# Shared key/value buffers in a gated mix of attention and a feed-forward net, and an earlier step for odd chunks' down weights

## The chip, the cores and the metric

The kernel runs on one core of one Trainium2 chip. A run's time is the device time of one execution, in microseconds (us), and less is better. The kernel before takes 601.78 us, the median of 3 runs (601.47 to 602.52). Each profiled execution also has a span, from its first to its last recorded instruction. The engines are TensorE (PE in the profile; its weight loads are PEld), VectorE (DVE), ScalarE (ACT), GpSimd (POOL) and SyncE (SP), which here only issues DMAs.

## The reference

Everything is in float32; x has 2048 rows of 512 columns.

```python
qkv = x @ wqkv                          # 32 heads of 16
idx = pos[:, None] - 2 * arange(8)      # 8 keys: this row and every second one behind it
logits = einsum("bhsd,bhswd->bhsw", q, k[idx]) * scale      # masked where idx < 0
o = einsum("bhsw,bhswd->bhsd", softmax(logits), v[idx])
a = o @ wo
b = (gelu(x @ w_gate) * (x @ w_up)) @ w_down                # 1792 hidden columns
g = sigmoid((x * gate_w).sum(-1))
out = g * a + (1 - g) * b
```

A row sees only keys at even distances, so even rows and odd rows never meet.

## The kernel before

The rows are split into two **parities** (`par` 0 and 1, even and odd rows, 1024 each), which go through the same stages one after the other: the projection of x to queries and keys; then `ffn(par)`, the feed-forward net in 14 chunks of 128 hidden columns (`f` = 0 to 13). In chunks 0 and 1 of `ffn` the pieces between the products are the projection to values (L130, banks `acc`); in later chunks they are the down projection of the two chunks before (L475, `down`). At the end stands the output projection (L693, L733 and after). By the trace the first projection lies at about 0 to 45 us, `ffn(0)` at 45 to 281, the second projection at 281 to 345, `ffn(1)` up to about 543, and the output projection behind it.

**Matmuls.** A float32 product is written as three matmuls of rounded halves: hi by hi, hi by lo, lo by hi. So each operand is split into `hi` (the rounded value) and `lo` (the rest). A chunk has seven block products of six matmuls each (L432, `product`), with sums of blocks in the place of an eighth product. Every matmul has a moving operand of 512 columns.

**The weights of a chunk.** The gate and up weights come as `raw` (SP, L360 and L361), VectorE makes block sums (L371 to L374, `combine`), and `operands` makes the halves in two groups, `g0` and `g1`: ScalarE writes minus hi into the lo half (L389), GpSimd issues a DMA that adds `raw` to it (L390, `g<-raw`, an accumulating DMA), and ScalarE writes hi (L394). The down weights go the same way in `down_w`: L418 on ScalarE, the accumulating DMA `d<-r` on GpSimd (L419), then L421 on ScalarE. For parity 1 `g0` comes back from DRAM (L385); `g1` and `d` are made again. `do` and `at(i, ...)` in `ffn` say at which of nine steps of a chunk's program each of these is written: step 0 is the chunk's head, step 8 its end.

**The hidden values.** ScalarE copies a product out of PSUM (`s`, L437), VectorE adds (`c`, L442), multiplies the gate and the up part (L446), ScalarE rounds (`hh`, L448), VectorE subtracts (`hl`, L449). `hh` and `hl` are the stationary operands of the down projection.

**Attention** runs on VectorE beside all this. A parity has four **units** (`u` = 0 to 3, 128 of the 512 channels), and a unit takes: keys and queries in (`load_kq`, L185), scores (L212 product and L215 sum, four times each, then L219, a minimum with the mask for the first rows, the last operation of a unit's scores), softmax (L226 to L236), the gate (L244, L246), values in (`mix`, L253), and the weighted sum (L260 to L268). It is written as a generator that is pulled forward a little at a time between the products, with lower priority. Keys lie in `2 * NP - 1` = 15 slots per partition (448 KB and 512 KB in two DMAs, L196 and L197), queries in 8 (512 KB, L193).

**Buffers.** `kq` (15 slots of keys and 8 of queries) and `v` (15 slots of values) have one buffer each. Unit 0 of a parity has its keys and queries written straight into `kq` by the projection (`take_first`, `shift`); the other units load them from DRAM. So a unit's keys can be loaded once the unit before has had its last L212, and a unit's values once the mix before is done.

**Order.** A scheduler orders each engine's queue from the program's order, priorities and a few written dependencies: `paced` makes an instruction wait for the last matmul written before it, `after` makes one instruction wait for another through a semaphore, `ordered` only fixes the order in a queue. An engine takes its queue strictly in order, so an instruction that waits holds all behind it. That goes for SP and GpSimd, which issue the DMAs, too.

Of the kernel before, what the change touches and what calls it, by code (L numbers as in the profile page):

```python
# [10 lines left out]
F32 = mybir.dt.float32  # L11
F32R = mybir.dt.float32r
AF = mybir.ActivationFunctionType
OP = mybir.AluOpType
AX = mybir.AxisListType

P = 128
S, D, F = 2048, 512, 1792
# [11 lines left out]
UC = 128  # L30
# [18 lines left out]
def tile_gated_mix(ctx: ExitStack, tc: tile.TileContext, xt, wqkv, wff, wo, out):  # L49
# [22 lines left out]
    zero = pool.tile([P, UC], F32, name="zero")  # L72
    nc.vector.memset(zero, 0.0)
    warm = zero.bitcast(mybir.dt.bfloat16)
    LAST = []
    idle = [bank("p") for _ in range(4)]
    for i in range(WARM):
        c = i // 4 % 2 * QW
# [57 lines left out]

    def take_first(par, ps, jj, copy):

        if par not in KQ:
            KQ[par] = pool.tile([P, 3 * NP - 1, UC], F32, name="kq")  # L140
        st = tl(next(stages))[:, :CU].rearrange("p (a d) -> p a d", a=2)
        two = ps.rearrange("p (a c d) -> p c a d", a=2, c=2)
        copy(KQ[par][:, NP - 1 + jj::NP], two[:, 0])
        copy(st, two[:, 1])
        for a, t in enumerate((KS[par, 0][1, W:], QS[par, 0][1])):
            nc.sync.dma_start(t.rearrange("(p j) d -> j p d", j=NP)[jj], st[:, a])

    def shift(par, queue, i, j):
        k = KQ[par][:, :2 * NP - 1]
        if not i:  # L150
            nc.gpsimd.memset(k[:1, :NP - 1], 0.0)
        for a, b in (1, P - 15), (P - 15, P):
            queue.dma_start(k[a:b, i:j], k[a - 1:b - 1, NP + i:NP + j])
# [28 lines left out]

    LG = {}

    def load_kq(par, u):  # L185
        hh, c = divmod(u, 2)
        kq = KQ[par] if not u else pool.tile([P, 3 * NP - 1, UC], F32, name="kq")
        k, q = kq[:, :2 * NP - 1], kq[:, 2 * NP - 1:]
        LG[par, u] = k, q
        if not u:  # L190
            return
        load_slots(k, KS[par, hh][c])
        nc.sync.dma_start(q, QS[par, hh][c].rearrange("(p j) d -> p j d", j=NP))  # L193

    def load_slots(t, src):
        nc.sync.dma_start(t[:, :NP - 1], src[:S // 2].rearrange("(p j) d -> p j d", j=NP)[:, 1:])  # L196
        nc.sync.dma_start(t[:, NP - 1:], src[W:].rearrange("(p j) d -> p j d", j=NP))  # L197

    def spans(t, jj):

# [6 lines left out]
    def scores(par, u):  # L207
        k, q = LG[par, u]
        lg = pool.tile([P, UH, NP, W], F32, name="lg", bufs=2)
        for jj in range(0, NP, 2):  # L210
            prod = pool.tile([P, 2, W, UC], F32, name="prod")
            paced(nc.vector.tensor_tensor(prod, spans(k, jj), q[:, jj:jj + 2, None, :].to_broadcast([P, 2, W, UC]),  # L212
                                          op=OP.mult))
            yield 2.3
            nc.vector.tensor_reduce(two_of(lg, jj), prod.rearrange("p j w (h d) -> p (j w) h d", d=DH), axis=AX.X,  # L215
                                    op=OP.add)
            yield 2.3
        first = lg[:1, :, :NP - 1, :W - 1]
        nc.vector.tensor_tensor(first, first, mask[:1, None, :NP - 1, :W - 1].to_broadcast([1, UH, NP - 1, W - 1]),  # L219
                                op=OP.min)  # L220
        LG[par, u] = lg

    def softmax(par, u):
# [25 lines left out]
    def mix(par, u, pause):  # L249
        lg = LG.pop((par, u))  # L250
        hh, c = divmod(u, 2)
        v = pool.tile([P, 2 * NP - 1, UC], F32, name="v")
        load_slots(v, VS[par, hh][c])  # L253
        yield pause
        tb = pool.tile([P, 2, BT * UC], F32, name="tb")
        for jj in range(0, NP, 2):
            if jj % BT == 0:
                o = pool.tile([P, 4, BT, 32], F32, name="o")
            prod = pool.tile([P, 2, W, UC], F32, name="prod")
            paced(nc.vector.tensor_tensor(prod.rearrange("p j w (h d) -> p (j w) h d", d=DH),  # L260
                                          spans(v, jj).rearrange("p j w (h d) -> p j w h d", d=DH),
                                          two_of(lg, jj)[:, :, :, None].to_broadcast([P, 2 * W, UH, DH]), op=OP.mult))
# [33 lines left out]
    def attention():  # L296
        units = [(0, u) for u in range(NU)] + [(1, u) for u in range(NU)]
        yield from need(0, 0)
        load_kq(0, 0)
        yield from scores(0, 0)  # L300
        load_kq(0, 1)
        yield from scores(0, 1)
        yield from need(0, 1)
        scored, mixed = 2, False
        for i, un in enumerate(units):
            if scored == i:
                yield from need(un[0], un[1] // 2 * 2)
                load_kq(*un)
                if un[1]:
                    yield LOAD  # L310
                yield from scores(*un)
                scored += 1
                mixed = False
            if un == (1, 0):
                load_kq(*units[scored])
            yield from softmax(*un)
            if un == (1, 0):
                yield from scores(*units[scored])
                scored += 1
                yield from need(un[0], 1)  # L320
            yield from gated(*un)


            to = units[scored] if scored < len(units) else None
            ahead = to and (to[0], to[1] // 2 * 2) in done
            if ahead:
                load_kq(*to)
            yield from mix(*un, LOAD if mixed else 0.0)
            done.add((*un, "o"))
            mixed = not ahead  # L330
            if ahead:
                yield from scores(*to)
                scored += 1
# [101 lines left out]
    def copy(ps):  # L435
        s = tl("s")
        COPIED[:] = [nc.scalar.activation(s, ps, AF.Copy)]  # L437
        return s
# [133 lines left out]
    def ffn(par):  # L572
# [3 lines left out]
        for f in range(FC):  # L576
# [10 lines left out]
            if f + 1 < FC:  # L587
# [7 lines left out]
                        at(3, down_split, g_)  # L595
                if f > 1:
                    steps = down_w(f)
                    at(2 if f > 2 else 4, next, steps, None)
                    at(7, next, steps, None)
            else:  # L600
                steps = down_w(f)
# [643 lines left out]
```

## Time and profile before

| | |
|---|---|
| median of 3 runs | 601.78 us (601.47 to 602.52) |
| the profiled execution, its own time | 602.86 us |
| its span | 601.0 us |
| TensorE busy | 591.8 us, 98% of the span, 2778 matmuls |
| VectorE busy | 531.1 us, 88% |
| ScalarE busy | 391.9 us, 65% |
| GpSimd busy | 89.3 us, 15% |
| moved by DMA | 134.18 MB, 223 GB/s on the mean |

The table's shares are means over the whole span. An engine's row in a timeline has the start, the duration, the engine, the line, the operation with what it writes and reads (`out<-in`), how many were merged into one row, and in brackets how long the engine sat idle before it and what ended that. A row of the list of waits has the engine, line and operand that waited, what it waited for, the total time in us, the number of waits and the longest. A row of the chain of waits is one step of the chain that ended last: start, duration, what. Matmuls are pipelined: the next starts before the one ahead ends, so the distance between starts, not the duration of one, says how fast they go.

### The profile page before, as it was taken

The numbers are of one execution on the slowest core, as the hardware profiler recorded it, in microseconds if no ns is written. First come the engines' busy times: TensorE is split into PE (matmuls) and PEld (weight loads), VectorE is DVE, ScalarE is ACT, GpSimd is POOL, SyncE is SP. The second block draws the span as 40 slices with busy tenths as digits, with TensorE's granted clock in tenths as the row PEclk, the third lists the DMA queues.
The fourth block names the chain that finished last, engine by engine and source line by source line (L and its number), as shares of the span: only waits on it lengthen the run. The fifth ranks groups of instructions, "written<-read, shape, count | busy, mean of one in ns | idle before, by whom it ended". The sixth has DMA issues, their size and how long they took to land.

```text
span 601.0 us, 8207 instructions
## 1 busy us (share of the span) xinstructions
PE 591.8 (98%) x2778; PEld 493.1 (82%) x2778; DVE 531.1 (88%) x618; ACT 391.9 (65%) x670; POOL 89.3 (15%) x121
## 2 busy tenths in 40 slices
PE   8999999999999999999999999999999999999997
PEld 6889987788888787888889988788888888888886
DVE  5997969999898897899989887999999988799862
ACT  6845657787678766787772375667667656885532
POOL 0501001111111111202026001111111111101300
PEclk9999999999999999999999999999999999999999
DMA  8789896999889989887879858597867877648924
GB/s 318 259 250 248 242 266 187 265 256 249 241 241 258 232 236 253 223 262 279 282 221 302 219 155 282 144 245 195 238 172 216 214 226 171 168 106 227 159 68 155
DMA packets 80449, 134.18 MB, mean 223 GB/s; under 512 B 8092, under 2 KB 46362, under 8 KB 80152
## 3 DMA queue, kind: packets, MB, share of 16 engines
q1 hardware_dynamic: 62890, 97.67, 50.3%
q0 software_dynamic: 12576, 32.97, 27.5%
q10 hardware_dynamic: 4942, 3.01, 1.6%
q8 instruction: 22, 0.36, 0.3%
q14 instruction: 19, 0.16, 0.1%
HBM read 68.30 MB, written 38.86 MB: 178 GB/s over the span
## 4 chain that ended last, share of the span: by engine, by line
PE 65%; DMA 12%; issue 11%; DVE 7%; ACT 2%; SPq 1%; POOL 1%; ACTq 0%; POOLq 0%; DVEq 0%
PE p L432 26%; PE p L475 9%; PE acc L475 8%; PE acc L760 6%; PE p L693 5%; PE p L760 5%; PE acc L130 4%; DMA d<-r 3%; DMA kq<-qs 3%; DMA ws<-g 3%; DVE prod L212 3%; PE acc L693 2%; DVE lg L215 1%; DMA g<-raw 1%; DMA vs<-hl 1%
## 5 line engine op out<-in xcount | busy, mean ns | idle before, releaser
L432 PE MATMUL p<-S,g 128*128 128x512 f32 x672 | 166.8, 390 | 0.5 <-ACT s L437 0.4
L432 PEld LDWEIGHTS p<-S,g 128*128 128x128 f32 x672 | 125.4, 188 | 27.2 <-ACT s L437 0.8
L432 PE MATMUL p<-A,g 128*128 128x512 f32 x504 | 127.2, 390 | 0.1
L432 PEld LDWEIGHTS p<-A,g 128*128 128x128 f32 x504 | 94.1, 188 | 20.6 <-DVE c L442 1.1
L212 DVE TENSOR_TENSOR prod<-kq 128x2048 f32<-128x2048 f32 x32 | 73.1, 2284 | 16.6 <-DMA kq<-qs 7.7
L390 POOL DMA_DIRECT2D g<-raw x40 | 34.6, 865 | 300.5 <-ACT g L389 230.1
L260 DVE TENSOR_TENSOR prod<-v,lg 128x2048 f32<-128x2048 f32 x32 | 72.9, 2277 | 2.3 <-DMA v<-vs 1.4
L215 DVE TENSOR_REDUCE lg<-prod 128x128 f32<-128x2048 f32 x32 | 73.0, 2281 | 0.2
L475 PE MATMUL p<-d,hh 128*128 128x512 f32 x224 | 68.1, 390 | 0.3 <-ACT hh L448 0.3
L475 PE MATMUL acc<-d,hh 128*128 128x512 f32 x224 | 60.7, 391 | 1.8 <-DMA d<-r 1.8
L475 PEld LDWEIGHTS acc<-d,hh 128*128 128x128 f32 x224 | 41.8, 188 | 11.6 <-DMA d<-r 2.6
L475 PEld LDWEIGHTS p<-d,hh 128*128 128x128 f32 x224 | 42.0, 188 | 9.5 <-ACT hh L448 0.8
L394 ACT ACTIVATE g<-raw 128x1024 fp32r<-128x1024 f32 (+1 forms) x40 | 39.5, 989 | 13.4 <-PE p L432 13.4
L389 ACT ACTIVATE g<-raw 128x1024 fp32r<-128x1024 f32 (+1 forms) x40 | 39.4, 985 | 10.9 <-PE p L760 4.6
L442 DVE TENSOR_TENSOR c<-p,s 128x512 f32<-128x512 f32 x56 | 38.0, 681 | 9.2 <-PE p L432 8.4
L448 ACT ACTIVATE hh<-c 128x512 fp32r<-128x512 f32 x56 | 35.0, 625 | 15.5 <-DVE c L446 15.0
L437 ACT ACTIVATE s<-p 128x512 f32<-128x512 f32 x56 | 33.1, 593 | 18.0 <-PE p L432 16.5
L475 PE MATMUL p<-d,hl 128*128 128x512 f32 x112 | 42.7, 390 | 1.0 <-DVE hl L449 1.0
L449 DVE TENSOR_TENSOR hl<-c,hh 128x512 fp32r<-128x512 f32 x56 | 38.3, 683 | 3.1 <-ACT hh L448 3.0
L446 DVE TENSOR_TENSOR c<-c 128x512 f32<-128x512 f32 x56 | 38.2, 682 | 2.1 <-ACT c L543 1.8
L264 DVE TENSOR_TENSOR prod<-prod 128x1024 f32<-128x1024 f32 x32 | 39.0, 1218 | 0.3
L491 ACT ACTIVATE rt<-p 128x512 f32<-128x512 f32 x48 | 28.2, 593 | 15.3 <-PE p L475 15.2
(180 smaller groups left out, 929.5 us busy)
## 6 DMA issues: line engine op xcount, KB each, us to landing
g<-raw POOLq DMA_DIRECT2D x27, 512.0 KB, 6.8
raw<-wff SPq DMA_DIRECT2D x42, 256.0 KB, 3.4
ws<-g SPq DMA_DIRECT2D x14, 768.0 KB, 6.1
g<-ws SPq DMA_DIRECT2D x14, 768.0 KB, 5.5
r<-wff SPq DMA_DIRECT2D x28, 256.0 KB, 4.3
d<-r POOLq DMA_DIRECT2D x24, 256.0 KB, 6.9
g<-raw POOLq DMA_DIRECT2D x13, 384.0 KB, 6.0
v<-vs SPq DMA_DIRECT2D x8, 512.0 KB, 5.7
```

The costliest lines, as they stand in the source:

```text
L212: paced(nc.vector.tensor_tensor(prod, spans(k, jj), q[:, jj:jj + 2, None, :].to_broadcast([P, 2, W, UC]), op=OP.mult))
L215: nc.vector.tensor_reduce(two_of(lg, jj), prod.rearrange("p j w (h d) -> p (j w) h d", d=DH), axis=AX.X, op=OP.add)
L260: paced(nc.vector.tensor_tensor(prod.rearrange("p j w (h d) -> p (j w) h d", d=DH), spans(v, jj).rearrange("p j w (h d) -> p j w h d", d=D ...
L264: nc.vector.tensor_tensor(prod[:, :, :4], prod[:, :, :4], prod[:, :, 4:], op=OP.add)
L389: nc.scalar.activation(lo, raw, AF.Copy, scale=-1.0)
L394: ins = nc.scalar.activation(hi, raw, AF.Copy)
L432: LAST[:] = [nc.tensor.matmul(ps, w_, a_, start=(start and kc == 0 and n == 0), stop=(kc == 1 and n == 2), skip_group_check=True)]
L446: nc.vector.tensor_tensor(ge, ge, up, op=OP.mult)
L449: nc.vector.tensor_tensor(hl_, ge, hh_.bitcast(F32), op=OP.subtract)
L475: ins = nc.tensor.matmul(pp, a[:, ts], w, start=(i == 0 and n == 0 and gr == 0), stop=(i == 1 and n == 2), skip_group_check=True)
L693: ins = nc.tensor.matmul(pa, a, b, start=(first and n == 0), stop=(last and n == 2), skip_group_check=True)
L760: return lambda *args, **kw: self.add(getattr(self.eng, name)(*args, **kw))
```

## The change

1. **One shared key buffer and one shared value buffer.** `KQ["a"]` (the tile `kq`) and `KQ["b"]` (the tile `v`) are allocated once and used by both parities. Unit 0's keys lie in `a`, those of the other units in `b`; values lie in `a`'s key slots, those of unit 3 in `b`. Queries lie in `a`'s query slots, except those of unit 1, which lie in a tile `tb` (in the orders below a load of keys therefore reads `v<-ks`, a load of values `kq<-vs`).
2. **A wait.** The loads of keys and queries of units 1 and 2 of parity 0 wait through `after` for `SCORED`, the L219 of the scores written last.
3. **An earlier place in the program.** `load_kq(1, 1)` is written right behind `load_kq(1, 0)`, ahead of unit (1, 0)'s scores; it was written behind them.
4. **Down weights.** In parity 0 the first step of `down_w` (the ScalarE write and the accumulating DMA) moves from step 2 of the chunk to step 0 for odd `f` from 3 on.

```diff
@@ take_first, shift
-        if par not in KQ:
-            KQ[par] = pool.tile([P, 3 * NP - 1, UC], F32, name="kq")
+        if "a" not in KQ:
+            KQ["a"] = pool.tile([P, 3 * NP - 1, UC], F32, name="kq")
...
-        k = KQ[par][:, :2 * NP - 1]
+        k = KQ["a"][:, :2 * NP - 1]
@@ load_kq, load_slots
+    def slots_of(other):
+        if not other:
+            return KQ["a"][:, :2 * NP - 1]
+        if "b" not in KQ:
+            KQ["b"] = pool.tile([P, 2 * NP - 1, UC], F32, name="v")
+        return KQ["b"]
+
     def load_kq(par, u):
         hh, c = divmod(u, 2)
-        kq = KQ[par] if not u else pool.tile([P, 3 * NP - 1, UC], F32, name="kq")
-        k, q = kq[:, :2 * NP - 1], kq[:, 2 * NP - 1:]
+        k, q = slots_of(u > 0), KQ["a"][:, 2 * NP - 1:]
+        if u == 1:
+            q = pool.tile([P, 2, BT * UC], F32, name="tb").rearrange("p a (b c) -> p (a b) c", c=UC)
         LG[par, u] = k, q
         if not u:
             return
-        load_slots(k, KS[par, hh][c])
-        nc.sync.dma_start(q, QS[par, hh][c].rearrange("(p j) d -> p j d", j=NP))
+        loads = load_slots(k, KS[par, hh][c])
+        loads.append(nc.sync.dma_start(q, QS[par, hh][c].rearrange("(p j) d -> p j d", j=NP)))
+        if not par and u < NU - 1:
+            for ins in loads:
+                after(ins, SCORED[-1])
@@ scores
-        nc.vector.tensor_tensor(first, first, mask[:1, None, :NP - 1, :W - 1].to_broadcast([1, UH, NP - 1, W - 1]),
-                                op=OP.min)
+        SCORED[:] = [nc.vector.tensor_tensor(
+            first, first, mask[:1, None, :NP - 1, :W - 1].to_broadcast([1, UH, NP - 1, W - 1]), op=OP.min)]
@@ mix
-        v = pool.tile([P, 2 * NP - 1, UC], F32, name="v")
+        v = slots_of(u == NU - 1)
@@ attention
                 if un[1]:
                     yield LOAD
+                else:
+                    load_kq(un[0], 1)
                 yield from scores(*un)
...
-            if un == (1, 0):
-                load_kq(*units[scored])
@@ ffn
-                    at(2 if f > 2 else 4, next, steps, None)
+                    at(4 if f == 2 else 0 if f % 2 and not par else 2, next, steps, None)
```

Three places in the engines' queues show what moves. In the changed file lines stand 8 to 11 lower: L390 is L401, L419 is L430, L212 is L223, L215 is L226, L219 is L230, L446 is L457, L449 is L460, L442 is L453, L196 and L197 are L207 and L208, L193 is L201.

**GpSimd, chunks 8 and 9 of parity 0.** In a row, `g1_1789` (before) or `g1_1788` (after) is chunk 8's second group; `g0_1872`, `g1_1923` (before) and `g0_1871`, `g1_1922` (after) are chunk 9's gate and up weights; `d_1899` and `d_1898` are the down weights of chunk 8, `d_2040` and `d_2002` those of chunk 9. Before:

```order
L390 DMA g1_1789<-raw_1618 128x1024
L390 DMA g0_1872<-raw_1746 128x768
L390 DMA g1_1923<-raw_1746 128x1024
L419 DMA d_1899<-r_1730 128x512
L390 DMA g0_2016<-raw_1875 128x768
L419 DMA d_2040<-r_1859 128x512
L390 DMA g1_2064<-raw_1875 128x1024
```

And in the changed kernel:

```order
L401 DMA g1_1788<-raw_1617 128x1024
L430 DMA d_1898<-r_1729 128x512
L401 DMA g0_1871<-raw_1748 128x768
L401 DMA g1_1922<-raw_1748 128x1024
L430 DMA d_2002<-r_1858 128x512
L401 DMA g0_2016<-raw_1874 128x768
L401 DMA g1_2061<-raw_1874 128x1024
```

The down weights of chunk 8, an even chunk, now go ahead of both groups of chunk 9, and those of chunk 9, an odd one, ahead of chunk 10's first group. Chunk 10's own down weights stay behind chunk 11's two groups in both kernels.

**VectorE, from the end of unit (0, 0)'s scores on.** `c`, `hl` and `d` belong to the feed-forward net and its weights; `prod` and `lg` to the scores, `m` to the softmax. Before:

```order
L219 TENSOR_TENSOR lg<-lg,mask 1x8x7x7
L226 TENSOR_REDUCE m<-lg 128x64
L228 TENSOR_TENSOR lg<-lg,m 128x512
L212 TENSOR_TENSOR prod<-kq 128x2048
L215 TENSOR_REDUCE lg<-prod 128x16x8
L446 TENSOR_TENSOR c<-c 128x512
L88 TENSOR_TENSOR d<-r,d 128x512
L371 TENSOR_TENSOR raw<-raw 128x2x256
L88 TENSOR_TENSOR d<-r,d 128x512
L442 TENSOR_TENSOR c<-p,s 128x512
L212 TENSOR_TENSOR prod<-kq 128x2048
```

And in the changed kernel:

```order
L230 TENSOR_TENSOR lg<-lg,mask 1x8x7x7
L237 TENSOR_REDUCE m<-lg 128x64
L239 TENSOR_TENSOR lg<-lg,m 128x512
L457 TENSOR_TENSOR c<-c 128x512
L88 TENSOR_TENSOR d<-r,d 128x512
L382 TENSOR_TENSOR raw<-raw 128x2x256
L223 TENSOR_TENSOR prod<-v,tb 128x2048
L88 TENSOR_TENSOR d<-r,d 128x512
L453 TENSOR_TENSOR c<-p,s 128x512
L382 TENSOR_TENSOR raw<-raw 128x256
L460 TENSOR_TENSOR hl<-c,hh 128x512
L453 TENSOR_TENSOR c<-p,s 128x512
```

The first product of unit (0, 1), which needs the loaded keys, moves from ahead of L446, L88 and L371 to behind them, and from there to the second product of this unit stand more operations of the feed-forward net than before.

**SP, the keys of unit (1, 1).** `ks_99` and `qs_101` are this unit's keys and queries in DRAM, `vs_100` and `vs_103` the values of parity 1; `r<-wff` are down weights, `g<-ws` chunk weights that come back. Before, they stand behind all stores of the values and the load of unit (1, 0)'s values:

```order
L162 DMA vs_103<-c 128x2x128
L196 DMA v<-vs_100 128x896
L197 DMA v<-vs_100 128x1024
L385 DMA g_3679<-ws_1185 128x1536
L196 DMA kq<-ks_99 128x896
L197 DMA kq<-ks_99 128x1024
L193 DMA kq<-qs_101 128x1024
L365 DMA r<-wff 128x512 x2
```

And in the changed kernel:

```order
L162 DMA vs_103<-hl 128x2x128
L207 DMA v<-ks_99 128x896
L162 DMA vs_100<-hh 128x2x128
L208 DMA v<-ks_99 128x1024
L162 DMA vs_103<-hl 128x2x128
L286 DMA os_98<-tb 32x4x128 x4
L422 DMA raw<-ws_1049 128x512
L162 DMA vs_100<-hh 128x2x128
L424 DMA raw<-wff 128x2x256
L201 DMA tb<-qs_101 128x1024
```

They now stand among the stores of the values, the queries behind the last stores from `tb` (`os_98`), whose place they take. The load of unit (0, 2)'s keys moves on SP too, the other way: it stood behind chunk 3's store of its first group (`ws_1185`), and stands behind chunk 4's (`ws_1332`).

More of the change, by code (lines that the diff above doesn't have):

```diff
@@ L74, in tile_gated_mix @@
     warm = zero.bitcast(mybir.dt.bfloat16)
-    LAST = []
+    LAST, SCORED = [], []
     idle = [bank("p") for _ in range(4)]
@@ L137, in take_first @@
     def take_first(par, ps, jj, copy):
-        if par not in KQ:
-            KQ[par] = pool.tile([P, 3 * NP - 1, UC], F32, name="kq")
+        if "a" not in KQ:
+            KQ["a"] = pool.tile([P, 3 * NP - 1, UC], F32, name="kq")
         st = tl(next(stages))[:, :CU].rearrange("p (a d) -> p a d", a=2)
         two = ps.rearrange("p (a c d) -> p c a d", a=2, c=2)
-        copy(KQ[par][:, NP - 1 + jj::NP], two[:, 0])
+        copy(KQ["a"][:, NP - 1 + jj::NP], two[:, 0])
         copy(st, two[:, 1])
@@ L191, in load_kq @@
             return
-        load_slots(k, KS[par, hh][c])
-        nc.sync.dma_start(q, QS[par, hh][c].rearrange("(p j) d -> p j d", j=NP))
+        loads = load_slots(k, KS[par, hh][c])
[3 more added lines that the diff above has]
+                after(ins, SCORED[-1])
     def load_slots(t, src):
-        nc.sync.dma_start(t[:, :NP - 1], src[:S // 2].rearrange("(p j) d -> p j d", j=NP)[:, 1:])
-        nc.sync.dma_start(t[:, NP - 1:], src[W:].rearrange("(p j) d -> p j d", j=NP))
+        return [nc.sync.dma_start(t[:, :NP - 1], src[:S // 2].rearrange("(p j) d -> p j d", j=NP)[:, 1:]),
+                nc.sync.dma_start(t[:, NP - 1:], src[W:].rearrange("(p j) d -> p j d", j=NP))]
     def spans(t, jj):
```

## The prediction

> **What bounds the kernel now.** I read the page first: the busy times and the granted clock.
>
> ```profile
> PE 591.8 (98%) x2778; PEld 493.1 (82%) x2778; DVE 531.1 (88%) x618; ACT 391.9 (65%) x670; POOL 89.3 (15%) x121
> PEclk9999999999999999999999999999999999999999
> ```
>
> TensorE is busy for 591.8 of 601.0 us at the full clock in every slice, and the change leaves every matmul as it is. So the time can only move by what TensorE waits. The list of TensorE's waits comes next.
>
> ```profile
> PE acc L475 <- DMA d<-r: 1.8, 2, 1.2
> PE p L79 <- DVE zero L73: 1.1, 1, 1.1
> PE p L475 <- DVE hl L449: 1.0, 1, 1.0
> PE acc L760 <- DVE A L760: 0.8, 1, 0.8
> PE p L432 <- ACT s L437: 0.4, 1, 0.4
> PE p L475 <- ACT hh L448: 0.3, 1, 0.3
> ```
>
> It names 5.4 us. L79 and L760 (1.9 us) are the start and the projection, which the change doesn't touch. A wait's full cost is seen in the distance between the starts of matmuls, and for that one needs their pace. The chain of waits gives it, and two long transfers beside it:
>
> ```profile
> 188.47 9.83 DMA d<-r
> ...
> 218.49 11.17 DMA d<-r
> ...
> 233.18 2.04 PE p L432 x9
> ```
>
> Nine matmuls of 512 columns in 2.04 us make 0.227 us each. Now TensorE's timeline around the four other waits, the one early in the feed-forward net of parity 0 first:
>
> ```profile
> 82.30 1.52 PE L432 MATMUL p<-S,g 128*128 128x512 f32 x6
> 84.25 1.65 PE L432 MATMUL p<-S,g 128*128 128x512 f32 x6 [0.42 <-ACT s L437]
> 85.74 0.61 PE L475 MATMUL acc<-d,hh 128*128 128x512 f32 x2
> ...
> 101.83 0.39 PE L475 MATMUL p<-d,hl 128*128 128x512 f32 x1
> 102.56 1.20 PE L475 MATMUL p<-d,hh 128*128 128x512 f32 x4 [0.34 <-ACT hh L448]
> 103.60 3.03 PE L432 MATMUL p<-A,g 128*128 128x512 f32 x12
> 106.47 0.61 PE L475 MATMUL p<-d,hl 128*128 128x512 f32 x2
> 107.05 1.66 PE L475 MATMUL acc<-d,hh 128*128 128x512 f32 x6
> 108.76 1.42 PE L432 MATMUL p<-S,g 128*128 128x512 f32 x5
> ```
>
> Six matmuls from 82.30 to 84.25 take 1.95 us where 6 times 0.227 is 1.36, so 0.59 are lost, and 0.13 in the next six: **place A, 0.7 us**. From 101.83 to 108.76 stand 1 + 4 + 12 + 2 + 6 = 25 matmuls, 5.67 us at that pace, in 6.93: **place B, 1.3 us**.
>
> ```profile
> 197.34 0.39 PE L475 MATMUL acc<-d,hh 128*128 128x512 f32 x1
> 198.34 1.43 PE L475 MATMUL acc<-d,hh 128*128 128x512 f32 x5 [0.62 <-DMA d<-r]
> ...
> 228.17 0.39 PE L475 MATMUL acc<-d,hh 128*128 128x512 f32 x1
> 229.71 1.43 PE L475 MATMUL acc<-d,hh 128*128 128x512 f32 x5 [1.15 <-DMA d<-r]
> ```
>
> One matmul in 1.00 us and one in 1.54: **place C, 0.8 us**, and **place D, 1.3 us**. These two wait for the accumulating DMAs of the chain above, issued at 188.47 and 218.49: the down weights of chunks 8 and 10.
>
> ```profile
> 378.43 0.73 PE L475 MATMUL p<-d,hl 128*128 128x512 f32 x2 [1.01 <-DVE hl L449]
> 379.03 1.66 PE L432 MATMUL p<-A,g 128*128 128x512 f32 x6
> 380.53 1.75 PE L432 MATMUL p<-S,g 128*128 128x512 f32 x7
> 382.42 0.96 PE L432 MATMUL p<-A,g 128*128 128x512 f32 x3
> ```
>
> Here 1.01 us of waiting, and 15 matmuls (3.40 us) in 3.99: **place E, 1.6 us**. A to E make 5.7 us: about the most that the change can win. From then on TensorE has no wait in the list.
>
> **The change, part by part.** *The wait on SCORED.* VectorE's and SP's timelines around the first loaded keys:
>
> ```profile
> 75.24 0.55 DVE L219 TENSOR_TENSOR lg<-lg,mask 1x392 f32<-1x392 f32 x1
> ...
> 81.80 2.29 DVE L212 TENSOR_TENSOR prod<-kq 128x2048 f32<-128x2048 f32 x1 [4.56 <-DMA kq<-qs]
> ...
> 86.33 0.68 DVE L446 TENSOR_TENSOR c<-c 128x512 f32<-128x512 f32 x1
> ```
>
> ```profile
> 71.80 0.32 SPq L196 DMA_DIRECT2D kq<-ks  x1
> ...
> 73.59 1.17 SPq L193 DMA_DIRECT2D kq<-qs  x1
> ```
>
> L219 ends at 75.79, so the loads start 4.0 us later than at 71.80. The first product came 10.0 us behind the first issue (81.80 less 71.80); it can then come at about 85.8. That looks like a loss of 4.0 us on VectorE, but its queue is reordered: L446, L88 and L371, which stood behind the product and the sum (4.6 us at 81.80 to 86.33), now stand ahead of them and fill the idle stretch. Attention is 4 us late; the feed-forward net, the one that TensorE waits for, is served earlier. On SP the waiting loads hold back the values' load and what follows, which before came only later anyway. Place B waits for `hh`, which hangs on VectorE's `c`, and should mostly go.
>
> Place A is another thing. ScalarE's copy L437 was late because of this:
>
> ```profile
> 81.89 0.39 ACT L160 ACTIVATE c<-acc 128x256 f32<-128x256 f32 x1 [2.88 <-DMA vs<-c]
> ```
>
> A small store of values was slow to land while the 1.4 MB of keys were in flight. Keys that start 4 us later still meet that store. So of A and B (2.0 us) I leave 0.5: a gain of **1.5**, with ends of 2.0 (both gone) and -1.5 (the 4 us come back as VectorE's backlog, less the idle stretch that is filled).
>
> *Down weights.* In GpSimd's queue chunk 8's accumulate moves ahead of two others, so place C goes, 0.8. But chunk 9's `g0` is now behind it and is issued about 1 us later; on TensorE it is needed before the down weights. No row shows its margin; I take 0.6 of new wait, between 0 (there is no wait on `g<-raw` now) and 1.5. C nets **0.2**. Chunk 10's down weights keep their place behind two accumulates. What shifts for them is TensorE's order, in which their first use comes about 1.4 us later (six matmuls, by the pace above), about as much as the wait: I leave 0.3 of 1.3, a gain of **1.0** (ends 1.3 and 0).
>
> How much one accumulate is worth is in the landings of GpSimd's DMAs, in order of all `d<-r`, then `g<-raw` issued from 104 to 122 us, then from 122 to 154:
>
> ```profile
> DMA to landing us min/median/max: 3.2/6.9/12.1
> ```
>
> ```profile
> DMA to landing us min/median/max: 9.6/10.1/10.6
> ```
>
> ```profile
> DMA to landing us min/median/max: 4.2/6.4/10.5
> ```
>
> The Trainium skill ("DMA: Bandwidth & Descriptors", section "Anatomy of one DMA — SWDGE (gpsimd) path") fits 2.0 us plus the bytes at 436 GB/s for a DMA of GpSimd, so 2.6 us for 256 KB. By that figure no accumulate that is moved back would be late, and the sum would be that of my first rival below; here the median is 6.9, so the trace speaks against it.
>
> *The price of crowding.* From 104 to 122 us the keys of unit (0, 2) were in flight, and accumulates took 10.1 us instead of 6.4. These keys now come a chunk later on SP, where chunk 5's `g0` meets them. Its landing can be 3.7 us later, less its margin, which no row shows; as TensorE has no wait on `g<-raw` at any place now, I take **1.2** of new wait, nearer to 0 than to 3.7. Chunks 6 and 8, whose `g0` now stands behind the odd chunk's down weights, get 0.3 each by the same reasoning as chunk 9 (ends 0 and 1.5): **0.6**.
>
> *Unit (1, 1).* VectorE's timeline:
>
> ```profile
> 369.36 2.29 DVE L212 TENSOR_TENSOR prod<-kq 128x2048 f32<-128x2048 f32 x1 [3.14 <-DMA kq<-qs]
> ```
>
> VectorE stood still for 3.14 us, with `hl` of place E queued behind. With the keys among the stores of the values they are there long before, the idle time goes, and `hl` would come up to 3.1 us earlier, more than the 1.6 that E costs. But without the stop the scheduler also puts this product earlier, ahead of work for TensorE. I leave 0.6: a gain of **1.0** (ends 1.6 and -0.5). In parity 1 chunk 2's down weights now follow later on GpSimd; **0.2** of new wait (0 to 1.5). The shared buffer also lets the projection write unit (1, 0)'s keys only after unit (0, 2)'s weighted sum; in the trace that ended some 10 us before, so 0, unless attention is 10 us late by then.
>
> *The sum.* Gains 1.5 + 0.2 + 1.0 + 1.0 = 3.7; new waits 1.2 + 0.6 + 0.2 = 2.0; net 1.7. The profiled execution took 602.86 us, 1.08 over the median of 601.78; 602.86 - 1.7 = 601.16 there, and **600.1** against the median.
>
> **Rivals.** *All gains and no new wait.* Margins on `g0` hold. For it: not one wait on `g<-raw` in the list. Against it: accumulates that already land up to 10.6 us after issue. 601.78 - (3.7 + 0.6 for chunk 9) = **597.5**.
>
> *Waits are only swapped.* The stalls at C and D belong to even chunks, while the edit moves odd ones, so it doesn't do there what it says; it only turns the order of a few accumulates, and the one put behind is late in the place of the other. Place D stays whole, and new waits grow to 3.0: gain 2.7 less 3.0, **602.1**; with smaller ones about 601.3. The Trainium skill has a rule for this ("DMA: Bandwidth & Descriptors", section "Issuing engines are not separate DMA queues"): DMAs of all issuers share the same 16 engines and interleave. The trace agrees (10.1 us beside the keys, 6.4 without).
>
> *Slower: the late keys hit chunk 5.* The 1.4 MB of unit (0, 2) and chunk 5's `g0` share the DMA engines, `g0` lands 3.7 us late, and chunk 6's, queued behind `d` of chunk 5, 1.5 late. New waits 3.7 + 1.5 + 0.8 = 6.0 against gains of 3.7: **604.1**; it decides from a margin of `g0` of chunk 5 under about 1.7 us.
>
> **Chances.** Forecast (599 to 600.5) 0.40; all gains 0.18; swapped 0.26; slower 0.16. A measurement of this kernel can tell about 0.2%, 1.2 us, from no change, so faster means under 600.6. Of the swapped case 0.21 is within, 0.03 slower and 0.02 faster. Of the slower case 0.03 ends within. That makes 0.60 faster, 0.24 same, 0.16 slower. The range goes from 597.0, a little below the first rival, to 603.0: it leaves out most of the slower case and a little below.
>
> **What would show it.** Right: no `d<-r` wait of over 0.3 us near 198 and 229; VectorE's idle time before unit (0, 1) filled with L446 and L88; no idle time before unit (1, 1)'s first product. Wrong: waits of L432 on `g<-raw` around chunks 5, 6 or 9 that add up to over 3 us, or waits on `hh` or `hl` around 100 to 115 us as long as before, since then VectorE's backlog was the 4 us of late keys and not the order of its queue.

## The result and the profile after

The changed kernel takes 600.12 us (599.15 to 600.48, 8 runs), the kernel before 601.62 us (600.5 to 602.54, 8 runs) beside it: a ratio of 0.9973, with a 95% interval of 0.9962 to 0.9984. That is 1.5 us or 0.25%, small but outside the noise of these runs, and the predicted 600.1 almost to the digit. The composition of the prediction was less good than its sum, and that is what the rest is about.

The profiled execution of the changed kernel took 600.41 us with a span of 598.5. First its busy times and clock, as on the page of before:

```profile
PE 591.7 (99%) x2778; PEld 493.0 (82%) x2778; DVE 529.3 (88%) x618; ACT 391.7 (65%) x670; POOL 89.2 (15%) x121
PEclk9999999999999999999999999999999999999999
```

TensorE does the same work at the same clock. Then the list of its waits:

```profile
PE p L79 <- DVE zero L73: 1.1, 1, 1.1
PE acc L771 <- DVE A L771: 0.7, 1, 0.7
PE p L443 <- DMA g<-raw: 0.7, 2, 0.5
PE p L486 <- ACT p L480: 0.5, 1, 0.5
PE p L771 <- ACT p L771: 0.3, 1, 0.3
```

The waits of places A to E (`s`, `hh`, `d<-r`, `hl`) are all gone from it; three new ones stand there (on `g<-raw`, on L480 and on ScalarE's L771). The timeline of TensorE shows two of them, at chunk 5 and at chunk 6:

```profile
131.21 0.39 PE L486 MATMUL p<-d,hl 128*128 128x512 f32 x1
132.11 0.73 PE L486 MATMUL p<-d,hh 128*128 128x512 f32 x2 [0.50 <-ACT p L480]
132.67 0.40 PE L486 MATMUL p<-d,hl 128*128 128x512 f32 x1
132.91 0.63 PE L443 MATMUL p<-A,g 128*128 128x512 f32 x2
134.01 1.20 PE L443 MATMUL p<-A,g 128*128 128x512 f32 x4 [0.47 <-DMA g<-raw]
...
156.27 0.74 PE L443 MATMUL p<-A,g 128*128 128x512 f32 x2 [0.20 <-DMA g<-raw]
```

From 131.21 to 134.01 stand six matmuls (1 + 2 + 1 + 2), 1.36 us at 0.227 each, in 2.80.

VectorE where the late keys were expected to leave a hole. Ahead of the first product of unit (0, 1), then at that of unit (1, 1):

```profile
76.13 0.55 DVE L230 TENSOR_TENSOR lg<-lg,mask 1x392 f32<-1x392 f32 x1
...
81.78 0.69 DVE L457 TENSOR_TENSOR c<-c 128x512 f32<-128x512 f32 x1 [3.66 <-ACT c L554]
82.79 0.69 DVE L88 TENSOR_TENSOR d<-r,d 128x512 fp32r<-128x512 f32 x1 [0.31 <-ACT d L117]
83.40 0.68 DVE L382 TENSOR_TENSOR raw<-raw 128x512 f32<-128x512 f32 x1
84.00 2.28 DVE L223 TENSOR_TENSOR prod<-v,tb 128x2048 f32<-128x2048 f32 x1
```

```profile
362.02 0.55 DVE L230 TENSOR_TENSOR lg<-lg,mask 1x392 f32<-1x392 f32 x1
362.50 2.27 DVE L223 TENSOR_TENSOR prod<-v,tb 128x2048 f32<-128x2048 f32 x1
```

L457, L88 and L382 stand ahead of the product, which starts at 84.00 instead of 81.80 (I had put it at 85.8). L457 waited 3.66 us for ScalarE, so the idle stretch was not filled; what counts is that L457 came 4.6 us earlier than at 86.33 before. Unit (1, 1)'s product waits for nothing.

ScalarE at place A, and the landing of the three stores of values that it issues from 74 to 77 us. The third fence gives, for the kernel before, the landing of the one store that its L160 waited for at place A (issued at 73.18); the fourth gives that of the same store in a second profile of before, of which more below (issued at 73.34):

```profile
77.44 0.39 ACT L160 ACTIVATE c<-acc 128x256 f32<-128x256 f32 x1 [0.97 <-PE acc L130]
```

```profile
DMA to landing us min/median/max: 2.0/2.1/3.0
```

```profile
DMA to landing us min/median/max: 8.7/8.7/8.7
```

```profile
DMA to landing us min/median/max: 5.2/5.2/5.2
```

In the changed kernel the keys are issued from 76.71 us on, and these stores land by 78.49, in 2.0 to 3.0 us, too early to be slowed by them. L160 waits for TensorE and not for a store. The next store, issued at 77.86, does meet the keys and takes 7.8 us, but TensorE loses nothing there. In the second profile of before the keys were in flight, too, and TensorE lost nothing at place A, as the store took 5.2 us and not 8.7.

Since this kernel's waits are few, one can add up all distances between matmul starts that exceed the pace of a back-to-back pair, all along the timeline. I do this for each profile and call it the **lost time**: 7.6 us in the first profile of before, 5.0 in that of the changed kernel. The difference of 2.6 agrees with that of the spans, 601.0 less 598.5.

### The profile page after: what moved, and what is told of

Read it like the earlier page. It is cut to its first block, busy times and chain, and to the rows that moved or that the text cites. A ratio compares the mean times of both kernels' runs of the same rounds, so it can differ in the third digit from the quotient of the medians.

```text
span 598.5 us, 8195 instructions
## 1 busy us (share of the span) xinstructions
PE 591.7 (99%) x2778; PEld 493.0 (82%) x2778; DVE 529.3 (88%) x618; ACT 391.7 (65%) x670; POOL 89.2 (15%) x121
## 4 chain that ended last, share of the span: by engine, by line
PE 90%; DMA 4%; issue 3%; DVE 1%; ACT 1%; SPq 0%; POOL 0%; POOLq 0%; ACTq 0%; DVEq 0%
PE p L443 41%; PE acc L486 11%; PE p L486 11%; PE acc L130 8%; PE acc L771 6%; PE p L771 6%; PE p L704 5%; DMA g<-raw 3%; PE acc L704 2%; DMA prod<-wqkv 1%; DVE g L771 0%; SPq L866 0%; DVE S L771 0%; DVE prod L275 0%; ACT rt L502 0%
## 5 line engine op out<-in xcount | busy, mean ns | idle before, releaser
L443 PE MATMUL p<-A,g 128*128 128x512 f32 x504 | 128.8, 391 | 0.7 <-DMA g<-raw 0.7
L401 POOL DMA_DIRECT2D g<-raw x40 | 34.6, 865 | 271.1 <-ACT g L400 195.6
L226 DVE TENSOR_REDUCE lg<-prod 128x128 f32<-128x2048 f32 x32 | 72.9, 2278 | 0.1
L486 PE MATMUL acc<-d,hh 128*128 128x512 f32 x224 | 59.0, 390 | 0.0
L271 DVE TENSOR_TENSOR prod<-kq,lg 128x2048 f32<-128x2048 f32 x24 | 54.6, 2274 | 1.0 <-PE acc L486 0.7
L453 DVE TENSOR_TENSOR c<-p,s 128x512 f32<-128x512 f32 x56 | 37.9, 680 | 8.3 <-PE p L443 7.4
L460 DVE TENSOR_TENSOR hl<-c,hh 128x512 fp32r<-128x512 f32 x56 | 38.2, 682 | 7.6 <-ACT hh L459 7.5
L457 DVE TENSOR_TENSOR c<-c 128x512 f32<-128x512 f32 x56 | 38.1, 681 | 6.4 <-ACT c L554 6.3
L130 PE MATMUL acc<-d,A 128*128 128x256 f32 (+1 forms) x288 | 37.9, 281 | 0.0
```

The lines of the kernel that those rows point to most:

```text
L130: LAST[:] = [nc.tensor.matmul(ps[:, :cn], a[:, t], w[:, c0:c0 + cn], start=(kc == 0 and n == 0), stop=(kc == KC - 1 and n == 2))]
L443: LAST[:] = [nc.tensor.matmul(ps, w_, a_, start=(start and kc == 0 and n == 0), stop=(kc == 1 and n == 2), skip_group_check=True)]
L457: nc.vector.tensor_tensor(ge, ge, up, op=OP.mult)
L460: nc.vector.tensor_tensor(hl_, ge, hh_.bitcast(F32), op=OP.subtract)
L486: ins = nc.tensor.matmul(pp, a[:, ts], w, start=(i == 0 and n == 0 and gr == 0), stop=(i == 1 and n == 2), skip_group_check=True)
```

## Experiments

Two theories stood against each other. **Theory 1**: each edit removes the stalls that it seems aimed at, so the wait on SCORED A and B, the down weights C and D, the loads of unit (1, 1) E. **Theory 2**: A to D all hang on the wait on SCORED, which reorders TensorE's and GpSimd's queues from chunk 2 on, and the fourth edit does nothing. The kernels ran in three sittings, each on a chip of its own, beside runs of before, whose median was 600.57 us (35 runs), 600.96 (29) and 601.55 (35) in the three.

The lost time by places, in us, worked out from each profile's timeline in that way (one execution each; the start and the first projection, 1.4 to 2.2 us in all, are left out). The columns are stretches of time, and not always the same wait stands in one: the 0.2 under C in the kernels with SCORED is a wait for VectorE ahead of chunk 9's first group, and what the kernels with SCORED for unit (0, 1) only lose under A lies at 90 us. In the changed kernel without SCORED the 1.1 under B is a wait for ScalarE at 111 us, and the 0.7 under E is one for chunk 2's down weights in parity 1, as is the 0.5 of the changed kernel:

| kernel | A | B | chunk 5 | chunk 6 | C | D | 232 to 340 us | E and after |
|---|---|---|---|---|---|---|---|---|
| before, first profile | 0.7 | 1.3 | 0 | 0 | 0.9 | 1.4 | 0 | 1.8 |
| before, second profile | 0 | 1.3 | 0 | 0 | 0 | 0.9 | 0 | 0.8 |
| changed, three profiles | 0 | 0.3 | 1.3 to 1.6 | 0.5 | 0.2 | 0 | 0.7 | 0 to 0.5 |
| down weights alone | 0 | 1.4 | 0 | 1.0 | 0 | 0.1 | 0 | 0.7 |
| SCORED alone | 0 | 0.3 | 1.4 | 0.3 | 0.2 | 0 | 0.7 | 1.6 |
| changed without SCORED | 4.4 | 1.1 | 0 | 0 | 0 | 0 | 0.2 | 0.7 |
| changed without down weights, two | 0 | 0.3 | 1.7, 1.4 | 0.6, 1.4 | 0.2 | 0 | 0.7 | 0 |
| SCORED for unit (0, 1) only | 0.3 | 0.5 | 0.9 | 0 | 0.2 | 0 | 0.7 | 0.2 |
| step 0 for all chunks | 0 | 0.3 | 1.9 | 0.3 | 0.1 | 0 | 0 | 0 |
| step 0 for even chunks | 0 | 0.3 | 2.1 | 0.6 | 0.1 | 0 | 0.4 | 0 |
| step 0 for all, SCORED for (0, 1) | 0.2 | 0.5 | 0.9 | 0.2 | 0 | 0 | 0 | 0 |

**The down weights alone**, put into the kernel before:

```diff
-                    at(2 if f > 2 else 4, next, steps, None)
+                    at(4 if f == 2 else 0 if f % 2 and not par else 2, next, steps, None)
```

> The kernel before with the fourth edit alone (odd chunks' down weights at step 0 in parity 0). Theory 1, each edit removes the stalls that it seems aimed at: the waits on d<-r near 198 and 229 us (places C and D, 2.1 us) go, so 1.2 to 2.1 us faster than before. Theory 2, the order of the accumulates of chunks 8 and 10 comes from the wait on SCORED, through the order of TensorE's queue, and not from this edit: GpSimd's queue keeps d of chunk 8 and d of chunk 10 behind two g<-raw, both waits stay, and the time is that of before within 0.4 us.

Measured: 600.68 us (599.67 to 601.84, 12 runs), ratio to before 1.0005 (0.9994 to 1.0017). GpSimd's timeline at chunk 8, first of this kernel, then of the one with SCORED alone:

```profile
186.53 0.86 POOL L390 DMA_DIRECT2D g<-raw  x1 [11.09 <-ACT g L389]
188.00 0.86 POOL L390 DMA_DIRECT2D g<-raw  x1 [0.61 <-DMA r<-wff]
189.00 0.86 POOL L419 DMA_DIRECT2D d<-r  x1
```

```profile
184.26 0.86 POOL L422 DMA_DIRECT2D d<-r  x1 [7.82 <-ACT d L421]
185.00 1.00 POOL L393 DMA_DIRECT2D g<-raw  x1
186.44 0.86 POOL L393 DMA_DIRECT2D g<-raw  x1 [0.43 <-ACT g L392]
```

The time of before, and chunk 8's `d` still behind the two accumulates: theory 1 falls for this edit. Yet the waits of C and D aren't in this profile either, against theory 2's wording: with chunk 10's `d` behind the same two accumulates, D is 1.4 us in the first profile of before, 0.9 in the second and 0.1 here. The landing lies at the edge of TensorE's need. Here it came no earlier than in the second profile of before (227.96 and 227.72 us), but TensorE came later, having lost 1.0 us at chunk 6, on a `g<-raw`: one wait took the place of another.

**SCORED alone**, put into the kernel before:

```diff
+        if not par and u < NU - 1:
+            for ins in loads:
+                after(ins, SCORED[-1])
```

> The kernel before with the second edit alone: the key loads of units 1 and 2 of parity 0 wait for L219. Theory 1: A and B go (2.0 us), C, D and E stay. Theory 2: A to D go (4.1 us), the new waits at chunks 5 and 6 come (about 2 us), and E stays, with VectorE idle some 3 us ahead of unit (1, 1)'s first product near 369 us: about 1 us more than the changed kernel, 600.5 to 601.5.

Measured: 601.73 us (600.84 to 602.43, 12 runs), ratio 1.002 (1.0009 to 1.003), **slower** than before. TensorE's two longest waits behind the start, and VectorE's wait ahead of unit (1, 1)'s first product:

```profile
...
PE p L478 <- DVE hl L452: 0.7, 1, 0.7
PE p L478 <- ACT p L472: 0.5, 1, 0.5
...
```

```profile
368.05 2.29 DVE L215 TENSOR_TENSOR prod<-kq 128x2048 f32<-128x2048 f32 x1 [2.91 <-DMA kq<-qs]
```

Here theory 2 is right on the places: A to D are gone, chunks 5 and 6 are there, E stays with its wait for the keys. In absolute time it erred by some 0.2 us. Against before it erred by more: 600.5 to 601.5 was meant to be at or a little under before's 601.6, and beside before on its own chip this kernel is 1.2 us slower. The profile of the down weights alone, from the same chip, has nothing at A and C and 0.1 at D, so there was less to win there than in the first profile; before itself has no profile from that chip. E is 1.6 us here and 0 in the profiles of all edits but the fourth: the shared buffers, with the third edit, take it away.

**The changed kernel without SCORED**:

```diff
-        if not par and u < NU - 1:
-            for ins in loads:
-                after(ins, SCORED[-1])
```

> The changed kernel without the wait on SCORED; the shared buffers, the place of unit (1, 1)'s loads and the down weights stay. Theory 1: places A and B come back (1.5 to 2 us), C and D stay away. Theory 2: C and D come back (0.8 and 1.3 us) as d of chunks 8 and 10 stand behind two g<-raw again, the new waits at chunks 5 and 6 (2.1 us in the changed kernel's profile) go, and unit (1, 1) still waits for nothing, so E stays away: about 600 to 601.2.

Measured: 602.61 us (601.06 to 605.93, 12 runs), ratio 1.005 (1.0033 to 1.0067). Both theories missed. ScalarE's and SP's timelines, then TensorE's timeline and the clock (the third number from the end in the row of a stretch, behind the busy times of the engines; then the DMA share and GB/s):

```profile
79.77 0.38 ACT L160 ACTIVATE c<-acc 128x256 f32<-128x256 f32 x1 [3.87 <-DMA vs<-c]
...
82.45 0.38 ACT L160 ACTIVATE c<-acc 128x256 f32<-128x256 f32 x1 [2.23 <-DMA vs<-c]
```

```profile
56.46 1.03 SPq L204 DMA_DIRECT2D v<-ks  x1
...
59.04 1.39 SPq L201 DMA_DIRECT2D tb<-qs  x1
70.28 0.38 SPq L368 DMA_DIRECT2D raw<-wff  x1
...
73.52 0.32 SPq L201 DMA_DIRECT2D kq<-qs  x1
```

```profile
85.69 4.36 PE L440 MATMUL p<-S,g 128*128 128x512 f32 x12 [2.81 <-ACT s L445]
```

```profile
86.00:89.00 3.00, 3.00 (x9) 2.33 (x9) 1.90 (x2) 3.00 (x6) 0.85 (x1) 0.57 0.84 253
89.00:92.00 3.00, 3.00 (x15) 2.49 (x14) 3.00 (x5) 2.28 (x4) 0.00 (x0) 1.00 1.06 250
```

With a buffer of its own, unit (0, 1)'s keys are loaded at 56 us, and nothing on VectorE holds them back. SP issues nothing from 60 to 70 us and then weights and unit (0, 2)'s queries close together, and the stores of values beside them make ScalarE wait 3.87 and 2.23 us. TensorE then stands for 2.8 us, and its clock drops for the next 3 us. So the wait on SCORED is what keeps place A shut once the buffers are shared. That the bunch of loads at 70 to 74 us is what slows the stores is argued from these rows and wasn't tried apart. Chunk 8's down weights stand behind two `g<-raw` again here, as theory 2 has it, and still C and D stay empty: TensorE had lost 5.5 us by then and first uses these weights at 201.23, and they had landed at 199.66.

**The changed kernel without the down weights**, twice:

```diff
-                    at(4 if f == 2 else 0 if f % 2 and not par else 2, next, steps, None)
+                    at(2 if f > 2 else 4, next, steps, None)
```

> The changed kernel without the fourth edit (odd chunks' down weights back at step 2). Theory 1: places C and D come back, 1.2 to 2.1 us slower than the changed kernel, so about 601.3 to 602.2. Theory 2: no wait on d<-r of over 0.3 us near 198 and 229, and the time of the changed kernel, 600.1, within 0.4 us.

Measured: 600.51 us (599.29 to 601.77, 12 runs), ratio to before 1.0001 (0.9991 to 1.0011), no wait at C or D. But before was about 1 us faster on that chip than on the others, and the changed kernel wasn't beside it. So both ran on another chip:

> The changed kernel a third time, as the other end for the three runs beside it. By the two measurements so far 1.0 to 1.5 us faster than before (ratio 0.9973 to 0.9986).

> The changed kernel without the fourth edit, again, now on one chip with the changed kernel. If the fourth edit does nothing here (theory 2), its time is the changed kernel's within 0.4 us. If the fourth edit is worth something after all (the first run of this one gave a ratio of 1.0001 to before), it is 0.6 to 1.5 us slower than the changed kernel.

Measured: the changed kernel 600.14 us (598.81 to 600.9), ratio 0.9979 (0.9965 to 0.9992); without the fourth edit 600.25 us (599.8 to 601.22), ratio 0.9983 (0.9968 to 0.9999), 12 runs each. The fourth edit is worth 0.1 us, nothing that can be told apart. What it does is to change chunk 6's wait: without it the first group is late there (0.6 and 1.4 us), with it the second (0.5). The third edit changes nothing once the buffers are shared: without it every engine's queue and its waits are the same. The scheduler seems to place unit (1, 1)'s loads by when their buffer is free, and that is the shared buffers' doing.

**Before and the changed kernel once more**, in the second sitting:

> The kernel before once more, for a second profile on the chip of the runs beside it. If places A to E are fixed by the order of the queues, they all show again, each within 0.4 us of the first profile (0.7, 1.3, 0.8, 1.3, 1.6). If those that wait for a DMA (A, C, D) hang on how fast it happened to land, they shrink or go while B, which waits for VectorE's backlog, stays.

> The changed kernel once more, beside the kernel before on this chip. If the gain is fixed by the order, 1.5 us faster than before again (ratio 0.9973 within 0.0015), with the new waits at chunks 5 and 6 (2.1 us) in the profile. If part of before's stalls is there only in some executions, the gain is smaller, 0 to 1 us.

Measured: the changed kernel 599.93 us (599.4 to 600.95, 12 runs) against 600.96 (599.11 to 602.85, 29 runs), ratio 0.9986 (0.9974 to 0.9998). The second profile of before, an execution of 599.96 us with a span of 598.0, has this list:

```profile
...
PE acc L475 <- DMA d<-r: 0.6, 1, 0.6
...
PE p L475 <- ACT hh L448: 0.4, 1, 0.4
PE p L432 <- DVE c L442: 0.2, 1, 0.2
```

A and C are gone without any change, D is down to 0.9, E to 0.8 (VectorE waited 2.13 us for the keys there, not 3.14); B is what it was. The lost time is 4.7 us against 7.6 and the span 3.0 us shorter. So the first profile showed an execution from the upper end of the range (602.86, the median 601.62 to 601.78). What went or shrank from one to the other hangs on DMA landings. Before's executions scatter more than the changed kernel's, 599.04 to 603.64 in the third sitting against 598.81 to 600.9; that the landings are the whole reason is likely, but two profiles don't show it.

**SCORED for unit (0, 1) only**, and the other two places for the down weights:

```diff
-        if not par and u < NU - 1:
+        if not par and u == 1:
```

> The changed kernel with the wait on SCORED for unit (0, 1) only; the loads of unit (0, 2) stand earlier on SP, and the order of all other engines stays. If the new waits at chunk 5 (131 to 134 us, 1.5 us) come from those keys landing beside chunk 5's g0, they shrink below 0.7 us, and the time is 0.5 to 1.3 us under the changed kernel's. If they come from ScalarE's queue (an exponential with two table loads ahead of chunk 5's L400), they stay, and the time with them.

Measured: 600.38 us (599.46 to 601.06, 11 runs), ratio 0.9985 (0.9974 to 0.9997), beside 599.93 for the changed kernel. Its TensorE at chunk 5:

```profile
132.95 0.74 PE L486 MATMUL p<-d,hh 128*128 128x512 f32 x2 [0.50 <-ACT p L480]
133.53 0.40 PE L486 MATMUL p<-d,hl 128*128 128x512 f32 x1
133.76 1.55 PE L443 MATMUL p<-A,g 128*128 128x512 f32 x6
```

The wait on `g<-raw` is gone from here, so that was the late keys of unit (0, 2). The landing of chunk 5's `g0`, first in the changed kernel, then in this one:

```profile
DMA to landing us min/median/max: 7.7/7.7/7.7
```

```profile
DMA to landing us min/median/max: 3.8/3.8/3.8
```

In the eight profiles in which unit (0, 2)'s keys wait for SCORED it takes 7.3 to 8.1 us, in both in which they don't 3.8. Chunk 6's wait is gone from this profile, too, but that isn't shown to be the keys: its accumulate still takes 8.6 us (9.0 in the changed kernel), beside a load of values, and 0.2 us are lost there again in the last kernel below. The wait on L480 stays to the hundredth. ScalarE's rows in the changed kernel, where it is busy without a gap from 122.74 us to behind L480:

```profile
123.36 1.28 ACT L241 ACT_TABLE_LOAD   x1
...
126.77 1.28 ACT L554 ACT_TABLE_LOAD   x1
...
131.46 0.60 ACT L480 ACTIVATE p<-rt 128x512 f32<-128x512 f32 x1
```

So that wait is ScalarE's own queue, in which the exponential of the softmax (L241) and its two table loads stand ahead of L480; no run moved them, so this cause is read from the rows alone. Of the 1.3 to 1.6 us at chunk 5, then, 0.9 are ScalarE's and 0.4 to 0.7 the keys'. By the medians no gain can be told: in this profile 0.3 us more stand at A and 0.2 at B, and the start happened to lose 0.4 more than in the changed kernel's of this sitting.

```diff
-                    at(4 if f == 2 else 0 if f % 2 and not par else 2, next, steps, None)
+                    at(4 if f == 2 else 0 if not par else 2, next, steps, None)
```

> The changed kernel with the first step of the down weights at step 0 for even chunks of parity 0, too. By theory 2 d of chunks 8 and 10 were no longer late, so the time is that of the changed kernel within 0.4 us; were their landing still at the edge in some executions, up to 0.7 us faster; if instead g0 of chunks 10 and 13, now behind them on GpSimd, is late, up to 1 us slower.

Measured: 599.19 us (598.05 to 600.18, 12 runs), ratio 0.9964 (0.9954 to 0.9975), 0.7 us under the changed kernel beside it. The gain is not where it was expected: C and D were already empty, and what is gone from this one profile is the wait at 285 us and what stood behind E in two of the changed kernel's three.

```diff
-                    at(4 if f == 2 else 0 if f % 2 and not par else 2, next, steps, None)
+                    at(4 if f == 2 else 0 if not f % 2 and not par else 2, next, steps, None)
```

> The changed kernel with the first step of the down weights at step 0 for the even chunks of parity 0 in the place of the odd ones. If the late ones are those of even chunks, chunk 10's above all, this does what moving all did (599.2, 0.7 under the changed kernel); if moving all gained only through odd and even together, it is at the changed kernel's time or above.

Measured: 599.81 us (598.38 to 601.22, 12 runs), ratio 0.9977 (0.9962 to 0.9992), 0.3 under the changed kernel's 600.14 and inside its scatter. Undecided: it doesn't show what moving all did, nor rule it out.

**Both better variants together** (step 0 for all, SCORED for unit (0, 1) only):

> Both of the better variants together: step 0 for all chunks of parity 0 from 3 on, and the wait on SCORED for unit (0, 1) only. If the early keys of unit (0, 2) take only the wait on g<-raw at chunk 5 away (0.7 us) and leave ScalarE's part (0.8), 0.3 to 0.8 us under the time with step 0 for all, about 598.6; if what they win there comes back around 89 and 104 us, as in the profile of the wait for unit (0, 1) only, no gain: 599.2.

Measured: 599.08 us (597.82 to 600.45, 12 runs), ratio 0.9962 (0.9947 to 0.9977), 1.1 us under the changed kernel beside it. TensorE's list:

```profile
...
PE p L486 <- ACT p L480: 0.5, 1, 0.5
PE p L443 <- DVE c L453: 0.2, 1, 0.2
```

This and step 0 for all are the fastest of these kernels. Between the two, which ran on different chips, nothing can be told.

## Why the prediction was right, and where it wasn't

**The bound** held: TensorE's work and clock are unchanged, and the spans of the two profiles differ by just what the lost time does.

**A and B** (gain 1.5 predicted): 1.7 between the two first profiles. For B the mechanism was right: the feed-forward operations go ahead of unit (0, 1)'s product and 0.3 us are left of 1.3. For A it was wrong: "Keys that start 4 us later still meet that store". They meet only a later one; the store that L160 needs took 3.0 us and landed at 76.97, where the keys are issued from 76.71 on. And A's 0.7 is there in one of the two profiles of before.

**C and D** (0.2 and 1.0): the waits went, and chunk 9's `g0`, for which I had left 0.6, was not late. The part that speaks of down weights named the right cause in GpSimd's and TensorE's orders, but put it under the fourth edit's heading; those orders come from the wait on SCORED, and the fourth edit alone gives 1.0005. The rival's remark that the edit doesn't do there what it says was the truth of it. D was mis-sized too: 1.3 from an execution that was late, 0.9 and 0.1 in others. Why it went is seen in the group of matmuls that uses chunk 10's down weights, whose second one needs the accumulate, in the second profile of before and in the changed kernel, and in the landing in the latter (issued at 218.46):

```profile
226.76 0.39 PE L475 MATMUL acc<-d,hh 128*128 128x512 f32 x1
227.76 1.43 PE L475 MATMUL acc<-d,hh 128*128 128x512 f32 x5 [0.61 <-DMA d<-r]
```

```profile
229.69 1.52 PE L486 MATMUL acc<-d,hh 128*128 128x512 f32 x6
```

```profile
DMA to landing us min/median/max: 9.4/9.4/9.4
```

The accumulate lands at nearly the same time in both, at 227.7 and 227.9. TensorE comes 2.9 us later: 1.4 by its order, as predicted, and the rest because it has lost more by then, 2.1 at chunks 5 and 6. By an estimate from these rows the order alone would have been enough, with 0.4 us to spare; the new waits widened that.

**E** (1.0): all of it went, 1.8 in one profile of before, 0.8 in the other, by the shared buffers and not by the third edit, which changes no queue. The scheduler's placing the product ahead of work for TensorE, for which I had kept 0.6 back, cost nothing that shows there.

**New waits** (2.0): the three profiles have 2.8 to 3.2. Chunk 5 lost 1.3 to 1.6 where I had 1.2, over half of it for a reason I had not seen (L480 behind ScalarE's table loads). The price of crowding was right in size, 3.9 us between chunk 5's `g0` with and without the late keys for 3.7, though it was read from two accumulates against four whose ranges overlap (9.6 to 10.6, 4.2 to 10.5); `g0`'s margin was larger than I had allowed for. That chunk 5's sum fits is luck, then. So it is at chunk 6, which lost 0.5 for 0.3: its `g0`, the one that I had priced, landed at 149.24 without a wait, and its second group was late. Chunk 8 lost none for 0.3. Not foreseen was the wait at 285 us on ScalarE's copies into the second projection's banks (L771), 0.5. Chunk 2's down weights in parity 1 lost 0 in the first profile and 0.5 in the next two, for 0.2.

**The sum**: the net of 1.7 stands against 1.5, 1.0 and 1.4 in the three measurements. That is luck in part, as errors met: the profile of before was of an execution 1.1 us above the median, which made the gains too large by up to 3 us, and the changed kernel's gains were more complete than I allowed. That the median moves by 1 to 1.5 although before's second profile loses less than the changed kernel's (4.7 against 5.0 to 5.3) fits before's wider scatter: the change would then win by the executions of before in which A and C occur and D and E are large. That is argued and not shown: how often they occur was not counted, since only two of before's executions have a profile. By the spans of these two the changed kernel's first profile is 2.5 us faster than one and 0.5 us slower than the other.

**The rivals**: the slower case did not happen, as chunk 5's `g0` was late by 0.5 us and not by 2. The swap of waits did happen in part: about 3 us of new waits took the place of 3.0 to 6.1. The condition of the slower case was named in the wrong place. What makes this change slower is a part of it left out: SCORED without the buffers (1.002), the buffers without SCORED (1.005). On the chip of these two all edits but the fourth were as fast as before (1.0001), and no faster.

**The signs**: two of the three signs of being right came, no wait on `d<-r` and no idle time before unit (1, 1). The third did not: VectorE's idle time before unit (0, 1) was not filled with L446 and L88, as L457 (the former L446) itself waited 3.66 us. Of the signs of being wrong none came; the waits on `g<-raw` add up to 0.7 us.

## What to carry to other kernels

Where an engine is 98% busy, add up every distance between its starts beyond the pace, and take that sum from two or more executions before pricing a stall: here a DMA that landed within a microsecond of its use was late in one execution and not in the next. Test the edits of a change one by one, as the one that names a resource need not be the one that moves it; here a wait on VectorE's scores set the order of GpSimd's accumulates, and of two edits that cost 1.2 and 2.0 us where the other is missing, the pair cost nothing on the same chip. A stall that is gone may also have been covered by a new one ahead of it, so look at when the data landed and not only at the wait. A buffer that becomes free earlier also frees its load to start earlier, and that load may then need a written wait.

## What the runs showed of the hardware

TensorE, after standing still for 2.8 us in the kernel without SCORED, was granted 0.57 of its clock from 86 to 89 us and full speed from 89 to 92 us: twelve matmuls from 85.69 us on took 4.20 us where 2.72 is their pace, so 1.5 us more, on top of the 3.0 that the wait cost. The Trainium skill ("TensorE: Matmul & The Clock Gate", section "What's actually happening") gives one idle window of about 3.4 us for the drop; here somewhat less was enough. A store of 128 KB landed in 2.0 to 3.0 us ahead of a key load and in 5.2 to 8.7 us beside one. An accumulate of 384 KB landed in 7.3 to 8.1 us with 1.4 MB of keys and queries issued 3 to 6 us ahead of it, and in 3.8 us with the keys issued 15 us ahead.
